# The second batch's products with w1 and w2 as seven block products per pair instead of eight

## The chip, the cores and the metric

The kernel runs on one core of one Trainium2 chip. The metric is the device time of one execution in microseconds; lower is better. Engines are named as in the profile: PE is TensorE (PEld its weight loads), DVE is VectorE, ACT is ScalarE, POOL is GpSimd, SP is SyncE, whose one queue issues every DMA.

## The reference

Attention with 16 clusters over 2 batches of 768 tokens and 8 heads, then two feed-forward layers without a softmax between them. What the change touches is the product of the attention's output x with w1 and w2 (512 by 1024 each), and what follows it:

```python
a = x @ w1                      # x is 1536 x 512: 768 rows per batch
b = x @ w2
h = a * b @ w3
x2 = h @ w_out
h2 = x2 @ w_in
g = h2 * np.clip(h2 + 3.0, 0.0, 6.0) / 6.0
return g @ w_out2
```

The kernel gets the weights as float64 and computes to float32 accuracy.

## The kernel before

Weights arrive as pairs of 32-bit words. A "conversion" (`conv_ops`, lines 691 to 727) makes float32 of 128 x 512 of them: a load of 512 KB into one of two `raw` buffers, a scaling on ScalarE (`c0`), a clamp on VectorE or GpSimd (`c1`), and three steps on VectorE (`c3`, `c4`, `c5`, lines 715, 719 and 723) into one of two `cvs` buffers.

A float32 product on PE is made of three matmuls in a rounded format: each operand is split into a rounded high part (a copy on ScalarE) and a low part (a subtraction on VectorE or GpSimd), and high·high, high·low and low·high are added in PSUM. So "a matmul of 128x384" below always comes in threes.

The program works in stages, in this order on PE. (1) Attention of both batches; into it are woven w3 times w_out (so that only one product `x2 = (a*b) @ (w3 w_out)` is left) and the first batch's products with w1 and w2 (`ab_mm`, line 838). (2) The first batch's x2 (`x2_mm`, line 955): 192 matmuls. (3) The second batch's products with w1 and w2 (`ab1_mm`, line 1006): for each of 8 column blocks `j` of 128, for two halves `hf` of the 768 tokens, for the two weights `w`, four blocks `kk` of the inner dimension, three matmuls each: 8 x 2 x 2 x 4 x 3 = 384 matmuls. ScalarE copies the product with w1 out of PSUM (`ab1_a`), VectorE multiplies the product with w2 by it (`ab1_g`, line 1017), ScalarE rounds the result and GpSimd or VectorE makes its low part (`ab1_h`, `ab1_l`). The split weights of six `j` were stored in DRAM during stage 1 (`abp`, 1 MB each) and are loaded again here; those of the last two stay in SBUF. (4) The second batch's x2, 192 matmuls. (5) The last layer in 16 panels, 8 per batch; each panel takes two column blocks of w_in as a 2 x 2 block matrix and does its product with x2 with seven block products of 6 matmuls each (`h_mm`, line 1281, Strassen's scheme in `PRO`), then 36 matmuls of 128x512 with w_out2 (`o_mm`, line 1325).

Strassen's scheme in stage 5 keeps running sums in one PSUM bank: product 0 is copied out by ScalarE (`snap`), and only then product 2 may add to that bank; after product 2 another copy, then product 4, copy, product 6; a second bank holds product 3 (copy) and product 5. So PE waits at each of these places for a copy, unless something lies between.

The order on every engine is decided at build time by a planner (`Plan.order`): each operation has durations, needs, rings of buffers it takes and drops, and a due time; the planner picks the earliest that can start, among equals the earliest due. At run time each engine works strictly through its list. `RUN_ON` says which engines an operation may use. `CV0, CVR` set the due times of the last stage's 32 conversions (16 of w_in, 16 of w_out2), whose results are stored to DRAM (`set_dram`) and fetched again by the panels.

Of the kernel before, what the change touches and what calls it, by code (L numbers as in the profile page):

```python
# [135 lines left out]
def cluster_attention_moe_kernel(  # L136
# [872 lines left out]
    def ab1_a(j, hf):  # L1009
        asb1[j, hf] = base.tile([128, HF], F32, tag="asb", name="asb", bufs=2)  # L1010
        copy_act(asb1[j, hf], W_.pop(("ab1", j, hf, 0))[:, 0:HF])

    def ab1_g(j, hf, first):
        ps, a = W_.pop(("ab1", j, hf, 1))[:, 0:HF], asb1[j, hf]
        if hf and first:
# [62 lines left out]
    CV0, CVR = 20.0, 3.4  # L1080
# [352 lines left out]
```

## Time and profile before

| | |
|---|---|
| median of 3 runs | 796.08 us (794.38 to 796.79) |
| profiled execution, its own time | 792.08 us |
| its span | 790.3 us |
| PE busy | 770.0 us (97%) |
| VectorE busy | 620.4 us (79%) |
| ScalarE busy | 510.8 us (65%) |
| GpSimd busy | 247.4 us (31%) |
| matmuls | 4519 |
| granted PE clock | full in every slice of the span |

The profiled execution took 4.0 us less than the median of the timed runs and 1.8 us more than its own span. A busy PE counts overlapping matmuls, so the rows of durations overlap; the spacing of starts is what a matmul costs in a stream.

### The profile page before, as it was taken

The numbers are of one execution on the slowest core, as the hardware profiler recorded it, in microseconds if no ns is written. First come the engines' busy times: TensorE is split into PE (matmuls) and PEld (weight loads), VectorE is DVE, ScalarE is ACT, GpSimd is POOL, SyncE is SP. The second block draws the span as 40 slices with busy tenths as digits, with TensorE's granted clock in tenths as the row PEclk, the third lists the DMA queues.
The fourth block names the chain that finished last, engine by engine and source line by source line (L and its number), as shares of the span: only waits on it lengthen the run. The fifth ranks groups of instructions, "written<-read, shape, count | busy, mean of one in ns | idle before, by whom it ended". The sixth has DMA issues, their size and how long they took to land.

```text
span 790.3 us, 12744 instructions
## 1 busy us (share of the span) xinstructions
PE 770.0 (97%) x4519; PEld 705.6 (89%) x4519; DVE 620.4 (79%) x1098; ACT 510.8 (65%) x1017; POOL 247.4 (31%) x286
## 2 busy tenths in 40 slices
PE   7799999999999999999999999999999999999998
PEld 5588887788899999999889999998889998889886
DVE  7998898999999898788985934678788676766742
ACT  5679997778877787767744522437675657555644
POOL 5733757343555454323222422211100110200100
PEclk9999999999999999999999999999999999999999
DMA  7443343333364542423346578573122213212102
GB/s 242 131 147 110 88 135 104 111 109 107 94 194 159 165 138 95 148 67 110 111 123 207 180 258 274 181 247 125 54 68 63 85 66 135 94 54 67 41 14 80
DMA packets 53135, 98.41 MB, mean 125 GB/s; under 512 B 4849, under 2 KB 31569, under 8 KB 51537
## 3 DMA queue, kind: packets, MB, share of 16 engines
q1 hardware_dynamic: 53072, 97.62, 38.8%
q8 instruction: 35, 0.57, 0.3%
q14 instruction: 28, 0.22, 0.1%
HBM read 73.43 MB, written 17.87 MB: 116 GB/s over the span
## 4 chain that ended last, share of the span: by engine, by line
PE 82%; DVE 8%; ACT 4%; issue 2%; DMA 2%; POOL 0%; SPq 0%; DVEq 0%; ACTq 0%; POOLq 0%
PE po L1325 17%; PE psh L1281 14%; PE psab L1006 8%; PE psab L838 8%; PE pst L494 7%; PE av L539 7%; PE ptr L519 7%; PE psw L769 5%; PE psx L955 4%; PE pa L388 2%; DVE cvs L719 1%; DVE den L503 1%; ACT p L511 1%; DVE pl L183 1%; PE ptkB L362 1%
## 5 line engine op out<-in xcount | busy, mean ns | idle before, releaser
L186 ACT ACTIVATE ph<-ptr 128x384 fp32r<-128x384 f32 x192 | 91.2, 487 | 44.4 <-PE ptr L519 43.3
L183 DVE TENSOR_TENSOR pl<-ptr,ph 128x384 fp32r<-128x384 f32 x192 | 103.0, 550 | 15.2 <-ACT ph L186 13.0
L503 DVE TENSOR_REDUCE den<-pst 128x1 f32<-128x768 f32 x96 | 91.2, 950 | 9.2 <-PE pst L494 7.6
L710 POOL TENSOR_SCALAR cvt<-cvt 128x512 f32<-128x512 f32 x72 | 53.9, 749 | 133.3 <-ACT cvt L186 123.8
L511 ACT ACTIVATE p<-pst,den 128x768 f32<-128x768 f32 x96 | 86.3, 898 | 9.5 <-DVE den L503 8.5
L519 PE MATMUL ptr<-id_f,p 128*128 128x128 f32 x576 | 88.9, 274 | 2.0 <-DVE pl L183 1.4
L838 PE MATMUL psab<-xT,abhl 128*128 128x384 f32 x384 | 85.7, 348 | 0.6 <-ACT asb L186 0.6
L519 PEld LDWEIGHTS ptr<-id_f,p 128*128 128x128 f32 x576 | 68.7, 140 | 12.1 <-DVE pl L183 2.3
L494 PE MATMUL pst<-kB,qB 128*128 128x512 f32 x192 | 70.3, 369 | 4.3 <-ACT p L511 4.0
L186 ACT ACTIVATE cvt<-raw 128x512 f32<-128x512 f32 x72 | 48.1, 668 | 35.5 <-DMA raw<-in_moe_w_out_dram 15.8
L539 PE MATMUL av<-ph,vs 128*128 128x384 f32 x192 | 69.7, 363 | 0.0
L838 PEld LDWEIGHTS psab<-xT,abhl 128*128 128x128 f32 x384 | 64.6, 189 | 2.5 <-ACT asb L186 1.1
L1006 PE MATMUL psab<-xT1s,abhl 128*128 128x384 f32 x384 | 66.7, 334 | 0.0
L1006 PEld LDWEIGHTS psab<-xT1s,abhl 128*128 128x128 f32 x384 | 66.6, 188 | 0.0
L494 PE MATMUL pst<-kA,qA 128*128 128x512 f32 x192 | 64.0, 338 | 0.8 <-issue 0.8
L539 PE MATMUL av<-pl,vs 128*128 128x384 f32 x192 | 64.7, 337 | 0.0
L715 DVE TENSOR_SCALAR cvs<-cvt 128x512 int32<-128x512 int32 x72 | 35.3, 492 | 27.6 <-DMA set<-cvs 21.4
L1303 ACT ACTIVATE tt<-m_sn,three 128x384 f32<-128x384 f32 x48 | 29.5, 617 | 42.2 <-DVE m_sn L1291 32.6
L186 ACT ACTIVATE m_sn<-psh 128x384 f32<-128x384 f32 x64 | 31.1, 485 | 35.8 <-PE psh L1281 35.7
L723 DVE SCALAR_TENSOR_TENSOR cvs<-cvt,cvs 128x512 int32<-128x512 int32 x72 | 53.6, 744 | 0.8
L769 PE MATMUL psw<-woh,wT 128*128 128x512 f32 x128 | 52.8, 419 | 0.0
L719 DVE SCALAR_TENSOR_TENSOR cvs<-raw,cvs 128x512 int32<-128x512 int32 x72 | 51.8, 722 | 0.9
(186 smaller groups left out, 1833.1 us busy)
## 6 DMA issues: line engine op xcount, KB each, us to landing
raw<-in_moe_w_dram SPq DMA_DIRECT2D x32, 512.0 KB, 3.8
m_gb<-set SPq DMA_DIRECT2D x64, 256.0 KB, 3.4
raw<-in_moe_w_out_dram SPq DMA_DIRECT2D x24, 512.0 KB, 3.8
raw<-in_moe_w_in_dram SPq DMA_DIRECT2D x16, 512.0 KB, 4.0
set<-cvs SPq DMA_DIRECT2D x32, 256.0 KB, 2.8
abp<-abhl SPq DMA_DIRECT2D x6, 1024.0 KB, 3.9
abhl<-abp SPq DMA_DIRECT2D x6, 1024.0 KB, 6.2
qn<-in_q_dram SPq DMA_DIRECT2D x16, 192.0 KB
```

The costliest lines, as they stand in the source:

```text
L183: nc.vector.tensor_tensor(out=out, in0=a, in1=b, op=ALU.subtract)
L186: nc.scalar.activation(out=out, in_=in_, func=AF.Copy, **kw)
L494: x = mm(out=psr[:, t, ks_], lhsT=TT["q" + nm, h][:, i, cs_], rhs=flat(TT["k" + nm, h])[:, ks_], start=st, stop=sp)
L503: done["mx", n] = [other_banks(nc.vector.tensor_reduce(out=dens[h][:, 0, c:c + 1], in_=psS[h, c], axis=AX.X, op=ALU.max, negate=True), ("S ...
L511: done["ex", n] = [other_banks(nc.scalar.activation(out=flat(p), in_=psS.pop((h, c)), func=AF.Exp, bias=d[:, 0, c:c + 1], accum_out=d[:, 1 ...
L519: nc.tensor.transpose(pt[:, blk(c)], pps[h, 3 * hf + c][:, blk(2 * s + i)], id_f)
L539: mm(out=t[:, 0:HF], lhsT=vs_t[h][:, 2 * s + i, :], rhs=x_[:, i, :], start=(s == 0 and i == 0 and n == 0), stop=(s == 2 and i == 1 and n = ...
L769: mm(out=ps, lhsT=wT[m, hf][:, a, blk(kk)], rhs=w_[hf][:, kk, :], start=(kk == 0 and n == 0), stop=(kk == 3 and n == 2))
L838: mm(out=ps[:, 0:HF], lhsT=s[:, w, a, blk(kk)], rhs=xT0[0][:, x_, kk, hf * HF:hf * HF + HF], start=(kk == 0 and n == 0), stop=(kk == KD - ...
L1006: mm(out=ps[:, 0:HF], lhsT=s[:, w, a, blk(kk)], rhs=x[:, x_, kk, hf * HF:hf * HF + HF], start=(kk == 0 and n == 0), stop=(kk == KD - 1 and ...
L1281: mm(out=ps[:, 0:HF], lhsT=left(p, l, a, kk), rhs=x[:, x_, kk, :], start=(st and kk == 0 and m == 0), stop=(kk == 1 and m == 2), skip_grou ...
L1325: mm(out=outs[b, c], lhsT=g[:, a, blk(c % 3)], rhs=w[:, w_, :], start=(first and a == 0 and w_ == 0), stop=(last and a == 1))
```

## The change

In stage 3 the two weights' column block `j` (a block of w1 and a block of w2, each cut into two halves of the inner dimension) and the second batch's x (cut into two halves of the inner dimension and two halves of the tokens) are treated as 2 x 2 block matrices and multiplied with the same seven products as in stage 5: 8 x 7 x 2 x 3 = 336 matmuls in place of 384. A "pair" below is one `j`, 42 matmuls.

For that, seven sums and differences of x's blocks are formed and split once, during stage 2 (`bx_sum`, `bx_hi`, `bx_lo`). Of the weights, float32 values are stored in stage 1 for all eight `j` (16 stores of 256 KB, straight from `cvs`) in place of six stores of split weights of 1 MB; they are fetched per pair (2 x 256 KB), four sums are formed on VectorE (`b_sum`), and seven operands are split in three pieces (`bl_hi` on ScalarE, `bl_lo` on VectorE). Out of PSUM, a pair now has four copies on ScalarE (`b_snap`), three additions on VectorE (`b_add` twice, `b_22`), and the two multiplications a*b on VectorE (`b_g0`, `b_g1`). The low part of the result is VectorE's alone (`"bl": "d"` in `RUN_ON`). The due times of the last stage's conversions move from 20 + 3.4 n to 110 + 3.9 n, behind these products; the preparation of the first batch's x2 for stage 5 moves behind them too, into stage 4. (No operation after stage 4 is itself changed.)

```diff
+    "bfs": "d", "b22": "d", "bg0": "d", "bl": "d", "bLl": "d",
...
-    ab_dram = [tc.dram_tile([128, 2048], F32, name=f"abp{j}") for j in range(J1 - 2)]
+    ab_dram = [tc.dram_tile([128, 2, 512], F32, name=f"abp{j}") for j in range(J1)]
...
+            lat=4.0 if key[0] == "set" else 2.0,
...
+    def ab_store(j, w):
+        nc.sync.dma_start(out=ab_dram[j][:, w], in_=cvo["ab", j, w])
...
+            op(("abp", j, w), "dma", 1.0, lambda j=j, w=w: ab_store(j, w), (("c5", "ab", j, w),), due=d - 0.3, lat=2.2)
             fop("abl", ("abl", j, w), {"p": 1.225, "d": 0.6}, lambda e, j=j, w=w: ab_lo(e, j, w), (("abh", j, w),),
-                due=d - 0.2, drop=("cvs",))
-        if j < J1 - 2:
-            op(("abp", j), "dma", 4.2, lambda j=j: nc.sync.dma_start(out=ab_dram[j], in_=flat2(abs_[j])),
-               (("abl", j, 0), ("abl", j, 1)), due=d + 1)
...
-                if (j, hf) in ((J1 - 2, 1), (J1 - 1, 0)):
-                    u += 0.5 if hf else -0.5
...
-    def xs_hi(kk):
-        if kk == 0:
-            xs1[0] = pool["t"].tile([128, 2, KD, S], F32R, tag="gA", name="xT1s")
-        copy_act(xs1[0][:, 0, kk, :], xT1[0][:, kk, :])
-
-    def xs_lo(e, kk):
-        sub_on(e, xs1[0][:, 1, kk, :], xT1[0][:, kk, :], xs1[0][:, 0, kk, :])
...
-    def ab1_mm(j, hf, w, kk):
-        if kk == 0:
-            bank(("ab1", j, hf, w), "psab")
-        ps, s, x = W_["ab1", j, hf, w], abs_[j], xs1[0]
-        for n, (a, x_) in enumerate(((0, 0), (0, 1), (1, 0))):
-            mm(out=ps[:, 0:HF], lhsT=s[:, w, a, blk(kk)], rhs=x[:, x_, kk, hf * HF:hf * HF + HF],
-               start=(kk == 0 and n == 0), stop=(kk == KD - 1 and n == 2))
...
+    XO = (0, 0), (1, 0), (1, 1), (0, 0), (0, 1), (1, 1), (1, 0)
+    XS = {3: ((0, 1), (0, 0)), 4: ((1, 1), (0, 1)), 5: ((1, 1), (0, 0)), 6: ((1, 0), (1, 1))}
...
+    PRO = ((0, 0, 0, True), (1, 1, 1, True), (0, 4, 5, False), (1, 5, 4, True), (0, 3, 3, False), (1, 2, 6, False),
+           (0, 6, 2, False))
...
+    def bx_sum(e, k_):
+        sub_on(e, xB(*XO[k_]), xB(*XS[k_][0]), xB(*XS[k_][1]))
+
+    def bx_hi(k_):
+        copy_act(bx[k_][:, 0], xB(*XO[k_]))
+
+    def bx_lo(e, k_):
+        sub_on(e, bx[k_][:, 1], xB(*XO[k_]), bx[k_][:, 0])
...
+    def b_fetch(j, w):
+        nc.sync.dma_start(out=bF[j % 2][:, 0:4:3] if w else bF[j % 2][:, 1:3],
+                          in_=ab_dram[j][:, w].rearrange("p (s f) -> p s f", s=2))
+
+    def b_sum(e, j, i):
+        x, y, o, g = ((0, 3, 4, ALU.add), (4, 1, 5, ALU.subtract), (1, 0, 6, ALU.subtract), (2, 5, 7, ALU.subtract))[i]
+        (nc.gpsimd if e == "pool" else nc.vector).tensor_tensor(
+            out=bF_at(j, o), in0=bF_at(j, x), in1=bF_at(j, y), op=g
+        )
...
+    def bl_hi(j, i):
+        t, f = b_part(j, i)
+        copy_act(t[:, :, 0], f)
+
+    def bl_lo(e, j, i):
+        t, f = b_part(j, i)
+        sub_on(e, t[:, :, 1], f, t[:, :, 0])
...
+    def b_mm(j, i, kk):
+        bk, l, r, st = PRO[i]
+        bk = 2 if i == 1 else bk
+        if kk == 0 and i in (0, 1, 3):
+            bank(("b", j, bk), "psab")
+        ps, t = W_["b", j, bk], bL[j % 2, l >= 3]
+        l = l if l < 3 else l - 3
+        for m, (a, x_) in enumerate(((0, 0), (0, 1), (1, 0))):
+            mm(out=ps[:, 0:HF], lhsT=t[:, l, a, blk(kk)], rhs=bx[r][:, x_, kk, :],
+               start=(st and kk == 0 and m == 0), stop=(kk == 1 and m == 2), skip_group_check=True)
...
+    def b_snap(j, i, nm):
+        t = bC[j, nm] = bs.pop(0)
+        copy_act(t, W_["b", j, PRO[i][0]][:, 0:HF])
...
+    def b_add(j, nm, i):
+        t = bC[j, nm]
+        tt(out=t, in0=t, in1=W_["b", j, 2 if i == 1 else 1][:, 0:HF], op=ALU.add)
...
+    def b_22(e, j):
+        t = bC[j, (1, 1)]
+        (nc.gpsimd if e == "pool" else nc.vector).tensor_tensor(out=t, in0=t, in1=bC[j, "s7"], op=ALU.add)
...
+    def b_g0(e, j):
+        t = bC[j, (0, 0)]
+        (nc.gpsimd if e == "pool" else nc.vector).tensor_tensor(out=t, in0=t, in1=bC[j, (1, 0)], op=ALU.mult)
...
+        tt(out=gb1[0][:, j, :], in0=bC[j, (1, 1)], in1=W_["b", j, 0][:, 0:HF], op=ALU.mult)
...
+    def b_l(e, j):
+        sub_on(e, gh1[0][:, 1, j, :], bC[j, (0, 0)], gh1[0][:, 0, j, :])
...
+    B0, BP = 33.6, 7.35
...
+                nd = [("bxl", r)] + ([("b", j, i, 0)] if kk else [("b", j, i - 1, 1)] if i else [("b", j - 1, 6, 1)] if j else
+                                     [("open", "bs")])
+                nd.append(("bll", j, 0 if l < 3 else (l - 1) // 2))
+                if kk == 0:
+                    nd += {2: [("bs", j, 0)], 4: [("bs", j, 2)], 5: [("bs", j, 3)], 6: [("bs", j, 4)]}.get(i, [])
+                end = i == 6 and kk
...
-    CV0, CVR = 20.0, 3.4
+    CV0, CVR = 110.0, 3.9
...
-        t0 = (22.0, D0 + 30.0)[b]
+        t0 = (X1 + 2.0, D0 + 30.0)[b]
```

What the change does to the lists of the engines, at three places.

VectorE in stage 3 (names: `asb`, `g1B` products of a and b, `cvs` conversions). Before, from one pair's last multiplication (`g1B`) past the next pair's two:

```order
L1017 TENSOR_TENSOR g1B<-asb,psab 128x384
L715 TENSOR_SCALAR cvs<-cvt 128x512
L719 SCALAR_TENSOR_TENSOR cvs<-raw,cvs 128x512
L723 SCALAR_TENSOR_TENSOR cvs<-cvt,cvs 128x512
L1017 TENSOR_TENSOR asb<-asb,psab 128x384
L715 TENSOR_SCALAR cvs<-cvt 128x512
L1017 TENSOR_TENSOR g1B<-asb,psab 128x384
L719 SCALAR_TENSOR_TENSOR cvs<-raw,cvs 128x512
L723 SCALAR_TENSOR_TENSOR cvs<-cvt,cvs 128x512
L715 TENSOR_SCALAR cvs<-cvt 128x512
L719 SCALAR_TENSOR_TENSOR cvs<-raw,cvs 128x512
L723 SCALAR_TENSOR_TENSOR cvs<-cvt,cvs 128x512
```

With the change, the second part of the instructions of one pair, up to the multiplication that closes it (`b_L`, `b_gv` operands from the weights, `b_sn` the copies out of PSUM, `gh1A` the low part of a*b):

```order
L184 TENSOR_TENSOR gh1A<-b_sn,gh1A 128x384
L184 TENSOR_TENSOR b_L<-b_gv,b_L 128x2x256
L1102 TENSOR_TENSOR b_sn<-b_sn,psab 128x384
L1067 TENSOR_TENSOR b_gv<-b_gv 128x256
L716 TENSOR_SCALAR cvs<-cvt 128x512
L1067 TENSOR_TENSOR b_gv<-b_gv 128x256
L720 SCALAR_TENSOR_TENSOR cvs<-raw,cvs 128x512
L1067 TENSOR_TENSOR b_gv<-b_gv 128x256
L1106 TENSOR_TENSOR b_sn<-b_sn 128x384
L1067 TENSOR_TENSOR b_gv<-b_gv 128x256
L1102 TENSOR_TENSOR b_sn<-b_sn,psab 128x384
L1119 TENSOR_TENSOR g1B<-b_sn,psab 128x384
```

A pair had 2 multiplications of its own and the rest were conversions; now it has 13 instructions of its own (four sums `b_gv`, three low parts of operands, three additions, two multiplications, one low part of the result) and about one conversion's three between them.

ScalarE in stage 3. Before (`asb` copies out of PSUM, `gh1A` the high part of the result, `cvt` a conversion's scaling):

```order
L186 ACTIVATE asb<-psab 128x384 x2
L186 ACTIVATE cvt<-raw 128x512
L186 ACTIVATE gh1A<-asb 128x384
L186 ACTIVATE asb<-psab 128x384
L186 ACTIVATE cvt<-raw 128x512
L186 ACTIVATE asb<-psab 128x384
L186 ACTIVATE gh1A<-asb 128x384
L186 ACTIVATE asb<-psab 128x384
L186 ACTIVATE cvt<-raw 128x512
L186 ACTIVATE asb<-psab 128x384
L186 ACTIVATE gh1A<-asb 128x384
```

With the change, from a pair's second and third copy on (`b_sn` copies out of PSUM, `b_w`, `b_L` high parts of the operands of the pair after the next):

```order
L187 ACTIVATE gh1A<-b_sn 128x384
L187 ACTIVATE b_sn<-psab 128x384 x2
L187 ACTIVATE cvt<-raw 128x512
L187 ACTIVATE b_sn<-psab 128x384
L187 ACTIVATE b_w_5321<-b_gv 128x3x256
L187 ACTIVATE b_L<-b_gv 128x2x256
L187 ACTIVATE b_sn<-psab 128x384
L187 ACTIVATE b_L<-b_gv 128x2x256
L187 ACTIVATE gh1A<-b_sn 128x384
L187 ACTIVATE b_sn<-psab 128x384 x3
L187 ACTIVATE cvt<-raw 128x512
```

The high part of the result `gh1A`, which waits for VectorE, now stands in the same list ahead of the copies on which PE's next products wait; before, no copy held up PE's running sum.

VectorE in stage 5, in the fourth panel. Before (`m_sn` copies out of PSUM, `tt` activations, `m_gv`, `m_whl`, `m_hl`, `m_gB` low parts, `m_gb` sums of fetched weights):

```order
L1291 TENSOR_TENSOR m_sn<-m_sn,psh 128x384
L1307 SCALAR_TENSOR_TENSOR tt<-tt,m_sn 128x384
L183 TENSOR_TENSOR m_gv<-tt,m_gv 128x384
L1182 TENSOR_TENSOR m_gb<-m_gb 128x256 x4
L1295 TENSOR_TENSOR m_sn<-m_sn 128x384
L1307 SCALAR_TENSOR_TENSOR tt<-tt,m_sn 128x384
L183 TENSOR_TENSOR m_w_5334<-m_gb,m_w_5334 128x512
L1291 TENSOR_TENSOR m_sn<-m_sn,psh 128x384
L183 TENSOR_TENSOR m_gv<-tt,m_gv 128x384
L1307 SCALAR_TENSOR_TENSOR tt<-tt,m_sn 128x384
L183 TENSOR_TENSOR x2f<-x2f 128x2x384
```

With the change, in the same panel:

```order
L1413 TENSOR_TENSOR m_sn<-m_sn,psh 128x384
L724 SCALAR_TENSOR_TENSOR cvs<-cvt,cvs 128x512
L1429 SCALAR_TENSOR_TENSOR tt<-tt,m_sn 128x384
L716 TENSOR_SCALAR cvs<-cvt 128x512
L720 SCALAR_TENSOR_TENSOR cvs<-raw,cvs 128x512
L184 TENSOR_TENSOR m_gv<-tt,m_gv 128x384
L724 SCALAR_TENSOR_TENSOR cvs<-cvt,cvs 128x512
L1311 TENSOR_TENSOR m_gb<-m_gb 128x256 x2
L1417 TENSOR_TENSOR m_sn<-m_sn 128x384
L1311 TENSOR_TENSOR m_gb<-m_gb 128x256
L716 TENSOR_SCALAR cvs<-cvt 128x512
L1429 SCALAR_TENSOR_TENSOR tt<-tt,m_sn 128x384
```

Each of the first panels now carries two conversions (`cvs`, `cvt`), where there were none. Of the 32 conversions of the last layer's weights, 5 stand before stage 2 in either list; with the change 3 stand in stage 2, 7 in stage 3, 5 in stage 4 and 12 in the first six panels of stage 5, where before none was left for stage 5.

## Rows read from the trace of the kernel before

**Rows 1.** The page, parts 1 and 4: busy time; the chain by engine.
```profile
PE 770.0 (97%) x4519; PEld 705.6 (89%) x4519; DVE 620.4 (79%) x1098; ACT 510.8 (65%) x1017; POOL 247.4 (31%) x286
...
PE 82%; DVE 8%; ACT 4%; issue 2%; DMA 2%; POOL 0%; SPq 0%; DVEq 0%; ACTq 0%; POOLq 0%
```

**Rows 2.** The chain in order of time: start us, length us, what.
```profile
434.87 66.57 PE psab L1006 x384
```

**Rows 3.** Busy us of each engine in stretches of the span.
```profile
core 0: us, PE busy (x) PEld busy (x) DVE busy (x) ACT busy (x) POOL busy (x), PEclk, DMA share, GB/s
400.50:434.80 34.30, 34.02 (x194) 33.23 (x193) 23.33 (x35) 14.74 (x24) 6.50 (x8) 1.00 0.53 162
434.80:501.30 66.50, 66.50 (x386) 66.50 (x385) 39.39 (x61) 24.22 (x43) 19.94 (x20) 1.00 0.70 229
501.30:534.50 33.20, 33.20 (x193) 33.20 (x192) 24.88 (x41) 14.88 (x23) 6.77 (x8) 1.00 0.70 229
...
550.20:644.50 94.30, 94.30 (x471) 84.93 (x470) 71.63 (x120) 59.52 (x106) 10.15 (x7) 1.00 0.22 72
```

**Rows 4.** Groups by form, 434.8 to 501.3: busy us, mean ns; idle.
```profile
L1006 PE MATMUL psab<-xT1s,abhl 128*128 128x384 f32 x384 | 66.7, 334 | 0.0
...
L180 POOL TENSOR_TENSOR gh1A<-asb,gh1A 128x384 fp32r<-128x384 f32 x8 | 11.8, 1469 | 18.4 <-ACT gh1A L186 18.4
```

**Rows 5.** Timeline of PE from 534: start, length, row, idle before.
```profile
534.55 2.24 PE L1281 MATMUL psh<-m_x,m_gB 128*128 128x384 f32 x12
...
540.51 1.32 PE L1281 MATMUL psh<-m_w,m_gB 128*128 128x384 f32 x6 [0.17 <-ACT m_sn L186]
...
542.72 2.24 PE L1325 MATMUL po<-m_w,m_whl 128*128 128x512 f32 x9
```

**Rows 6.** VectorE groups by form, 400 to 790 us.
```profile
L1182 DVE TENSOR_TENSOR m_gb<-m_gb 128x256 f32<-128x256 f32 x64 | 25.1, 420 | 0.7 <-DMA m_gb<-set 0.3
...
L723 DVE SCALAR_TENSOR_TENSOR cvs<-cvt,cvs 128x512 int32<-128x512 int32 x27 | 20.0, 741 | 0.6
L719 DVE SCALAR_TENSOR_TENSOR cvs<-raw,cvs 128x512 int32<-128x512 int32 x27 | 19.7, 732 | 0.6
L1291 DVE TENSOR_TENSOR m_sn<-m_sn,psh 128x384 f32<-128x384 f32 x32 | 17.5, 547 | 2.6 <-PE psh L1281 1.7
...
L715 DVE TENSOR_SCALAR cvs<-cvt 128x512 int32<-128x512 int32 x26 | 11.4, 439 | 26.2 <-DMA set<-cvs 21.4 <-POOL cvt L710 4.8
...
L183 DVE TENSOR_TENSOR m_hl<-m_gb,m_hl 128x512 fp32r<-128x512 f32 x7 | 4.8, 689 | 0.1
```

**Rows 7.** Timeline of VectorE from 619.6 us.
```profile
619.65 0.55 DVE L1307 SCALAR_TENSOR_TENSOR tt<-tt,m_sn 128x384 f32<-128x384 f32 x1
620.12 0.94 DVE L183 TENSOR_TENSOR x2f<-x2f 128x768 f32<-128x768 f32 x1
...
621.93 0.41 DVE L1182 TENSOR_TENSOR m_gb<-m_gb 128x256 f32<-128x256 f32 x1
622.26 0.95 DVE L183 TENSOR_TENSOR m_whl<-x2f,m_whl 128x768 fp32r<-128x768 f32 x1
623.13 0.55 DVE L183 TENSOR_TENSOR m_gv<-tt,m_gv 128x384 fp32r<-128x384 f32 x1
```

**Rows 8.** ScalarE groups by form, 434.8 to 790 us.
```profile
L186 ACT ACTIVATE m_sn<-psh 128x384 f32<-128x384 f32 x64 | 31.1, 485 | 35.8 <-PE psh L1281 35.7
...
L186 ACT ACTIVATE cvt<-raw 128x512 f32<-128x512 f32 x18 | 12.0, 669 | 22.9 <-DMA raw<-in_moe_w_out_dram 10.6 <-DMA raw<-in_moe_w_in_dram 8.3 <-DVE g1B L1017 3.6
...
L186 ACT ACTIVATE m_hl<-m_gb 128x512 fp32r<-128x512 f32 x13 | 8.1, 621 | 2.0 <-DMA m_gb<-set 1.7 <-PE po L1325 0.2
...
L186 ACT ACTIVATE m_gA<-x2f 128x768 fp32r<-128x768 f32 x4 | 3.2, 831 | 0.0
```

**Rows 9.** VectorE busy us (times) on line 723 in stretches.
```profile
0.00:400.50 400.50, 33.58 (x45) 1.00 0.42 129
...
534.50:790.00 255.50, 0.00 (x0) 1.00 0.21 72
```

More of the change, by code (lines that the diff above doesn't have):

```diff
@@ L876, in cluster_attention_moe_kernel @@
                        due=d + AR * kk / 16, take=("m",) if kk == 0 else (),
-                       drop=("hl",) if hf and w and kk == KD - 1 and j < J1 - 2 else ())
+                       drop=("hl",) if hf and w and kk == KD - 1 else ())
                 if w == 0:
@@ L888, in cluster_attention_moe_kernel @@
     op("xdone", "pe", 0.0, lambda: None,
-       [("ab", j, hf, 1, KD - 1) for j in (J1 - 2, J1 - 1) for hf in range(2)], due=105, drop=("x",))
+       [("ab", J1 - 1, hf, 1, KD - 1) for hf in range(2)], due=105, drop=("x",))
     pool, Whl = {}, []
@@ L1009, in ab1_a @@
[L1009 to L1015, printed above, removed]
+    BLK = {(i, j): (slice(2 * i, 2 * i + 2), slice(j * HF, j * HF + HF)) for i in range(2) for j in range(2)}
+    XO = (0, 0), (1, 0), (1, 1), (0, 0), (0, 1), (1, 1), (1, 0)
+    XS = {3: ((0, 1), (0, 0)), 4: ((1, 1), (0, 1)), 5: ((1, 1), (0, 0)), 6: ((1, 0), (1, 1))}
@@ new lines, in b_open_w16, with b_open_gv, b_open_hl @@
+    def b_open_w16():
+        t = base.tile([128, 4096], F32R, tag="w16", name="b_w16")
+        for i in range(2):
+            bL[i, 0] = t[:, 1536 * i:1536 * i + 1536].rearrange("p (o a f) -> p o a f", o=3, a=2)
+    def b_open_gv():
+        for _ in range(2):
+            t = pool["t"].tile([128, 1536], F32, tag="gv", name="b_gv", bufs=2)
+            bF.append(t.rearrange("p (s f) -> p s f", s=6))
+    def b_open_hl():
+        for i in range(2):
+            t = base.tile([128, 2048], F32R, tag="hl", name="b_L", bufs=2)
+            bL[i, 1] = t.rearrange("p (o a f) -> p o a f", o=4, a=2)
@@ new lines, in b_open_sn @@
+    def b_open_sn():
+        t = base.tile([128, 8, HF], F32, tag="x1b", name="b_sn")
+        for i in range(8):
+            bs.append(t[:, i])
+    allab = [("ab", J1 - 1, hf, 1, KD - 1) for hf in range(2)]
+    for nm, fn, take, need in (
+        ("bx", b_open_x, ("x",), ["xdone"]), ("bw", b_open_w16, ("w16",), [("Wl", KH - 1)]),
+        ("bg", b_open_gA, ("gA",), [("x2", 0, 0, KD - 1, J1 - 1)]), ("bh", b_open_hl, ("hl", "hl"), allab),
+        ("bv", b_open_gv, ("gv", "gv"), ["top"]), ("bs", b_open_sn, ("x1b",), [("bxl", k_) for k_ in range(7)]),
+    ):
+        op(("open", nm), "pe", 0.0, fn, need, due=-100, take=take)
@@ new lines, in xB @@
+    def xB(i, j):
+        r, c = BLK[i, j]
+        return xT1[0][:, r, c]
+    def bx_sum(e, k_):
[4 more added lines that the diff above has]
+        sub_on(e, bx[k_][:, 1], xB(*XO[k_]), bx[k_][:, 0])
+    for k_ in range(7):
+        d = T(6 + 3.5 * k_)
+        nd = [("pm", KD + i) for i in range(KD)]
+        if k_ >= 3:
+            need = {3: [("bxl", 0)], 4: [("bxs", 3)], 5: [("bxl", 2), ("bxs", 4)], 6: [("bxl", 1), ("bxs", 5)]}[k_]
+            fop("xsum", ("bxs", k_), {"d": 0.87, "p": 1.8}, lambda e, k_=k_: bx_sum(e, k_), nd + need, due=d)
+            nd = [("bxs", k_)]
+        op(("bxh", k_), "act", 0.75, lambda k_=k_: bx_hi(k_), nd + [("open", "bx" if k_ < 3 else "bg")], due=d + 0.1)
+        fop("xwl", ("bxl", k_), {"d": 0.87, "p": 1.8}, lambda e, k_=k_: bx_lo(e, k_), (("bxh", k_),), due=d + 0.2,
+            drop=("x1b",) if k_ == 6 else ())
@@ L1016, in ab1_g, with b_g1, b_h @@
+    gb1 = [None]
+    def b_g1(j):
+        if j == 0:
             gb1[0] = base.tile([128, J1, HF], F32, tag="gb", name="g1B")
-        tt(out=gb1[0][:, j, :] if hf else a, in0=a, in1=ps, op=ALU.mult)
-    def ab1_h(j, first):
-        if first:
+        tt(out=gb1[0][:, j, :], in0=bC[j, (1, 1)], in1=W_["b", j, 0][:, 0:HF], op=ALU.mult)
+        bs.append(bC.pop((j, (1, 1))))
+    def b_h(j):
+        if j == 0:
             gh1[0] = pool["t"].tile([128, 2, J1, HF], F32R, tag="gB", name="gh1A")
-        copy_act(gh1[0][:, 0, j, :], asb1[j, 0])
@@ L1057, in g1_hi @@
+    op("bend", "pe", 0.0, lambda: None, [("bl", j) for j in range(J1)] + [("bg1", j) for j in range(J1)], due=T(B0),
+       drop=("x1b",))
     def g1_hi(jp):
```

140 lines of the change are left out of this document (81 added, 59 removed).

## The prediction

> **What bounds the kernel now.** The page first: PE is busy 97% of the span and holds 82% of the chain that ended last [rows 1]. A busy share alone proves nothing, so next the chain in order of time. Through stage 3 it is one unbroken piece of PE, 384 matmuls in 66.57 us [rows 2]; that is 173.4 ns each, though one lasts 334 ns [rows 4], since they overlap. The stretches say the same: PE busy 66.50 of 66.50 us in stage 3, 33.20 of 33.20 in stage 4, 94.30 of 94.30 in six panels of stage 5; only at stage 2's start is a little idle (34.02 of 34.30) [rows 3]. So stages 2 to 5 are PE's, and a matmul less there is worth its 173.4 ns for as long as nothing else becomes late. Third, the engines beside it: in stage 3 VectorE is busy 39.39 and ScalarE 24.22 of 66.50 us; in stage 5 VectorE already 71.63 of 94.30 us [rows 3]. VectorE is the one to watch.
>
> **What is removed.** 48 of 384 matmuls: 48 x 173.4 ns = **8.3 us**; what is left takes 336 x 173.4 = 58.3 us, 7.28 us per pair.
>
> **The copies inside a pair.** Now PE may start product 2 only when product 0 has been copied, and so at four places in 42 matmuls. A product is 6 x 0.1734 = 1.04 us; a copy takes 0.485 us on ScalarE [rows 8]. Between a product's end and the one that waits lies one other product, 1.04 us of cover, so the copy may begin up to about half a microsecond late. ScalarE's pair is four copies (1.94), high parts of operands (0.83 for 768 columns, 2 x 0.62), one of the result (as a copy, 0.49) and about one conversion's scaling (0.67) [rows 8], together 5.2 of 7.28 us: enough time, but a copy can stand behind a 0.83 us operation. The nearest row is the first panel of stage 5, the only place where the seven products run today with nothing between them: from 534.55 to 542.72 us [rows 5], 8.17 us for 42 matmuls that cost 7.28, so 0.89 us lost, with a wait for ScalarE's copy shown at 540.51. There ScalarE had activations and x2's last copy as well, and VectorE stands in the way twice, since product 3 takes the bank that product 1's addition must have left; the new pair gives product 1 a bank of its own. Bounds for eight pairs: nothing (all copies under the other product) and 8 x 0.89 = 7.1 us. I take 0.3 us per pair, a third of the row because two of its causes are gone: **+2.4 us**.
>
> **VectorE in stage 3.** By the list, a middle pair has 13 instructions of its own: four sums of 256 columns (0.42 each), six of 384 columns (0.55), a low part of 768 columns (0.95) and two of 512 (0.69) [rows 6, 7], together 7.3 us, and with one conversion (0.44 + 0.73 + 0.74 = 1.91) 9.2 us. That is more than PE's 7.28. But durations are not what they cost in a row: on VectorE 384 columns of 0.55 us started 0.47 after one another, 256 columns of 0.41 gave way after 0.33, 768 columns of 0.95 after 0.87 [rows 7]; each next one starts 0.08 us before the last has ended. Sixteen of them then take 9.2 - 1.3 = 7.9 us, thirteen without a conversion 6.3. The stage's list, between the first and the last product, has 110 instructions with seven conversions: 64 us by durations, 55.5 by the spacing, against PE's 58.3. So VectorE is full but not over, because the operands of the first two pairs are made in stage 2 and those of a ninth do not exist. The worst pairs fall 0.6 us behind. That matters for one instruction: ScalarE's `gh1A`, which waits for VectorE's product, stands ahead of the copy of product 2. That copy is needed 3.1 us into the next pair, so VectorE may lag some 1.5 us before PE feels it. I take **0**; the upper bound is the sum by durations, 64 us plus the 0.7 that the first pair's multiplication comes after its last matmul, about 65 us, that is +6.7 and then instead of the copies' term.
>
> Here a rule of the Trainium skill speaks against the change. The page "VectorE: DVE Perf Modes", section "The DRAIN you can't avoid", says that the next operation does not start until the pipeline of the one before has emptied. By it VectorE's durations add up in full, and the stage would be the rival B below; the spacing in [rows 7] disagrees for operations of just this kind.
>
> GpSimd is no help and no harm there: of the low parts that it made before (1.47 us each [rows 4]) none is left to it, only the conversions' clamps.
>
> **Stages 1, 2 and 4.** Stage 1 has 16 stores of 256 KB in place of six of 1 MB, and about as many conversions in the new list as the 45 on VectorE before 400.5 us [rows 9]; the stores leave earlier in a conversion than before, so nothing queues on SP for longer. I take 0, within 1 us either way. In stage 2 VectorE gets 30 us by the spacing against 33.3 of PE, in order of need; the stage's first matmuls wait for VectorE as now. In stage 4 its list has 44 instructions, 32.4 us by durations and 28.9 by the spacing, in 33.2 us: again **0**, at most 1 us at the hand-over to stage 5, whose first panel waits for an addition that stands behind this list.
>
> **Stage 5.** Before, all conversions were done by 534.5 us [rows 9]; now 12 of 32 lie in its first six panels, two in each. VectorE was busy 71.63 / 6 = 11.9 of a panel's 15.7 us, idle 3.8 [rows 3]; two conversions less their overlaps add 2 x (1.91 - 0.24) = 3.3, so 15.3 of 15.7. If the idle time is all usable, it costs nothing. If the waits that made up those 3.8 us (for ScalarE, mostly) stay as they are, each of six panels is 3.3 us longer, 20 us. An engine that has more to do comes later to its waits and finds them over, so I am near the lower end, but the additions that free PE's bank now stand behind steps of 0.73 us: 0.3 us for each of six panels, about **+1.9 us**. The conversions are in time: 20 are done when the stage begins, enough for five panels, and two panels' worth of work brings the next panel's four, while the sixth panel's four are needed only after five panels.
>
> **The sum.** -8.3 + 2.4 + 0 + 0 + 1.9 = -4.0 us. On the profiled execution's own 792.08 us (span 790.3 and 1.8 around it) that is 788.1; that execution lies 4.0 us below the median of the runs shown, 796.08, and against this median the same difference gives **792.1 us**.
>
> **Rivals.**
> A, the forecast: the saving is kept but for a few small waits, 789 to 795 us. For it speaks that VectorE and ScalarE stay under PE by the spacing everywhere. 0.53.
> B, VectorE sets the pace in stage 3: it costs its durations there, the stage takes 65 us, and -8.3 + 6.7 + 1.9 = +0.3: 796.4 us, no change. For it: 9.2 against 7.28 us by durations, and a conversion's steps are longer still than a subtraction of as many columns (0.73 and 0.74 against 0.69 [rows 6]). Against it: rows 7's spacing. 0.20.
> C, slower: in stage 5 the waits of VectorE do not shrink. The place is the first six panels; the price, if half of the 3.8 us stays, is 15.3 + 1.9 - 15.7 = 1.5 us a panel, 8.9 us for six; -8.3 + 2.4 + 8.9 = +3.0: 799.1 us. It decides from the point where VectorE's work and remaining waits pass 15.7 us, that is from 0.4 us of waits; PE breaks even with the saving at about 1.0 us a panel. For it: VectorE's 76% without any conversion. Against it: PE waited for nothing in those panels, so there was slack in the waits. 0.14.
> D, everything is hidden: -8.3, 787.8 us. 0.13.
>
> **How the numbers follow.** About 0.3% (2.4 us) is what a measurement of this kernel can tell from no change. Faster than 793.7: four fifths of A (0.42) and D, 0.55. Within: the rest of A, most of B, a little of C, 0.30. Slower than 798.5: most of C, a little of B, 0.15. The predicted time is A's, 792.1. A's own range is 789 to 795; to leave out no more than 2 in 10 it is widened to D's 787.5 and past C's centre to 799.5.
>
> **What the profile after would show.** Stage 3 as 336 matmuls in 59 to 62 us, with short waits of PE for ScalarE's copies and none for VectorE; VectorE above 85% busy there. If B, PE's waits are in the products after `gh1A`, or for operands' low parts, and VectorE has no idle time. Stage 4 unbroken at 33.2 us. Panels of 15.7 to 16.2 us in the first six, 15.7 after. If C, the first six are 17 us and more, with PE waiting for VectorE's additions or for sets that land late. The prediction is wrong above all if ScalarE's list, where the copies stand behind operations that wait for VectorE or for a load, stops PE for longer than 0.3 us a pair.

## The result and the profile after

The change is faster: median 786.97 us (785.95 to 788.87), ratio to the kernel before 0.9901, interval 0.9877 to 0.9926. Two repeats on other occasions gave 0.9917 and 0.9913. The ratio times the 796.08 us that the prediction used is 788.2; the median itself lies 0.5 us under the stated range's lower end of 787.5.

First the page of the changed kernel, parts 1 and 4, to be read against [rows 1]:

```profile
PE 762.6 (97%) x4471; PEld 698.3 (89%) x4471; DVE 659.7 (84%) x1193; ACT 534.7 (68%) x1061; POOL 258.2 (33%) x277
...
PE 83%; DVE 9%; ACT 4%; issue 3%; DMA 1%; ACTq 0%; POOL 0%; DVEq 0%; SPq 0%; POOLq 0%
```

PE is as full as before and holds as much of the chain; VectorE went from 79% to 84%. The shares say that the character of the kernel is unchanged, not where time was won. That is in the stretches, cut at the first matmul of each stage (stages 2, 3, 4, the first panel of stage 5, the next six panels), against [rows 3]:

```profile
core 0: us, PE busy (x) PEld busy (x) DVE busy (x) ACT busy (x) POOL busy (x), PEclk, DMA share, GB/s
400.04:433.31 33.27, 33.27 (x193) 33.27 (x193) 29.49 (x46) 16.58 (x27) 8.77 (x3) 1.00 0.34 108
433.31:491.69 58.38, 58.38 (x337) 58.22 (x337) 52.52 (x106) 34.95 (x66) 11.12 (x8) 1.00 0.46 145
491.69:524.98 33.29, 33.29 (x194) 33.29 (x194) 27.41 (x44) 19.25 (x29) 14.03 (x4) 1.00 0.44 144
524.98:536.74 11.76, 9.41 (x43) 8.77 (x43) 10.49 (x19) 6.86 (x15) 1.52 (x2) 0.85 0.90 286
536.74:631.20 94.46, 94.46 (x471) 84.92 (x471) 89.85 (x152) 64.64 (x116) 19.96 (x17) 1.00 0.45 144
```

Stage 3 is 58.38 us, all of it PE's. The panels after the first take 94.46 us for six, as before, though VectorE is busy 89.85 us there, where the same six panels of before had 73.34:

```profile
542.72:637.18 94.46, 94.46 (x471) 85.05 (x471) 73.34 (x126) 60.08 (x108) 10.20 (x7) 1.00 0.21 68
```

One row of the change is new: the first panel, 11.76 us with PE busy 9.41 and a granted clock of 0.85. The next view is PE's waits from stage 3 to the end (us in total, times, longest); there are two, and both lie in that panel:

```profile
PE psh L1403 <- DVE m_sn L1413: 2.1, 1, 2.1
PE psh L1403 <- ACT m_sn L187: 0.3, 1, 0.3
```

PE's timeline there shows the wait in brackets, and behind it two rows of six matmuls that take 1.9 us from start to start in place of 1.04:

```profile
524.98 2.24 PE L1403 MATMUL psh<-m_x,m_gB 128*128 128x384 f32 x12
527.48 1.31 PE L1403 MATMUL psh<-m_x1b,m_gB 128*128 128x384 f32 x6 [0.26 <-ACT m_sn L187]
530.89 2.09 PE L1403 MATMUL psh<-m_x1b,m_gB 128*128 128x384 f32 x6 [2.10 <-DVE m_sn L1413]
532.77 2.03 PE L1403 MATMUL psh<-m_x,m_gB 128*128 128x384 f32 x6
534.64 1.22 PE L1403 MATMUL psh<-m_w,m_gB 128*128 128x384 f32 x6
535.70 1.20 PE L1403 MATMUL psh<-m_x,m_gB 128*128 128x384 f32 x6
```

Stretches of one microsecond say why (the granted clock is the third column from the end): it stays full during the wait and falls to half behind it, that is 1.2 in place of 2.4 GHz.

```profile
529.00:530.00 1.00, 0.00 (x0) 0.00 (x0) 1.00 (x2) 0.00 (x0) 0.23 (x1) 1.00 1.02 375
531.00:532.00 1.00, 1.00 (x4) 1.00 (x5) 0.66 (x3) 1.00 (x3) 0.00 (x0) 0.57 0.98 340
532.00:533.00 1.00, 1.00 (x5) 1.00 (x4) 0.68 (x2) 0.84 (x2) 0.49 (x1) 0.50 1.06 380
```

The addition that PE waited for is late because VectorE stood still for 5.37 us, 8 us earlier, at a conversion's first step that wants a result buffer whose store has not landed. VectorE's timeline:

```profile
512.74 1.28 DVE L724 SCALAR_TENSOR_TENSOR cvs<-cvt,cvs 128x512 int32<-128x512 int32 x2
513.94 1.48 DVE L184 TENSOR_TENSOR m_gB<-m_gb,m_gB 128x1280 fp32r<-128x1280 f32 x1
515.34 0.68 DVE L184 TENSOR_TENSOR m_hl<-m_gb,m_hl 128x512 fp32r<-128x512 f32 x1
515.94 0.68 DVE L184 TENSOR_TENSOR m_gB<-m_gb,m_gB 128x512 fp32r<-128x512 f32 x1
521.99 0.43 DVE L716 TENSOR_SCALAR cvs<-cvt 128x512 int32<-128x512 int32 x1 [5.37 <-DMA set<-cvs]
...
530.29 0.54 DVE L1413 TENSOR_TENSOR m_sn<-m_sn,psh 128x384 f32<-128x384 f32 x1
```

Both buffers had been finished by 514.02 us, together, and SP's queue issues their stores (L1289) only at 516.86, behind fetches (L1306, L1323) whose buffers VectorE's low parts at 513.94 and 515.34 had to free first:

```profile
515.44 0.89 SPq L1306 DMA_DIRECT2D m_gb<-set  x2
516.42 0.38 SPq L1323 DMA_DIRECT2D m_gb<-set  x1
516.86 0.90 SPq L1289 DMA_DIRECT2D set<-cvs  x2
```

So VectorE waits for a store that waits, in SP's order, for VectorE.

### The profile page after: what moved, and what is told of

It is laid out like the page before. It is cut to its first block, busy times and chain, and to the rows that moved or that the text cites. A ratio compares the mean times of both kernels' runs of the same rounds, so it can differ in the third digit from the quotient of the medians.

```text
span 785.5 us, 12835 instructions
## 1 busy us (share of the span) xinstructions
PE 762.6 (97%) x4471; PEld 698.3 (89%) x4471; DVE 659.7 (84%) x1193; ACT 534.7 (68%) x1061; POOL 258.2 (33%) x277
## 4 chain that ended last, share of the span: by engine, by line
PE 83%; DVE 9%; ACT 4%; issue 3%; DMA 1%; ACTq 0%; POOL 0%; DVEq 0%; SPq 0%; POOLq 0%
PE po L1447 17%; PE psh L1403 15%; PE psab L843 8%; PE pst L495 7%; PE av L540 7%; PE psab L1093 7%; PE ptr L520 7%; PE psw L771 5%; PE psx L956 4%; PE pa L389 3%; DVE den L504 1%; DVE pl L184 1%; DVE cvs L720 1%; ACT p L512 1%; PE ptkB L363 1%
## 5 line engine op out<-in xcount | busy, mean ns | idle before, releaser
L711 POOL TENSOR_SCALAR cvt<-cvt 128x512 f32<-128x512 f32 x72 | 75.8, 1056 | 192.6 <-ACT cvt L187 181.2
L720 DVE SCALAR_TENSOR_TENSOR cvs<-raw,cvs 128x512 int32<-128x512 int32 x72 | 49.6, 694 | 0.4
L495 PEld LDWEIGHTS pst<-kB,qB 128*128 128x128 f32 x192 | 36.1, 188 | 10.1 <-ACT p L512 7.7
L716 DVE TENSOR_SCALAR cvs<-cvt 128x512 int32<-128x512 int32 x72 | 33.5, 470 | 12.2 <-POOL cvt L711 6.7
L1447 PE MATMUL po<-m_hl,m_gv 128*128 128x512 f32 x162 | 43.7, 393 | 0.0
```

The lines of the kernel that those rows point to most:

```text
L495: x = mm(out=psr[:, t, ks_], lhsT=TT["q" + nm, h][:, i, cs_], rhs=flat(TT["k" + nm, h])[:, ks_], start=st, stop=sp)
L711: (nc.gpsimd.tensor_scalar if e == "pool" else ts)(out=tf, in0=tf, scalar1=H_MAX, scalar2=-H_MAX, op0=ALU.min, op1=ALU.max)
L1447: mm(out=outs[b, c], lhsT=g[:, a, blk(c % 3)], rhs=w[:, w_, :], start=(first and a == 0 and w_ == 0), stop=(last and a == 1))
```

## The experiments

The table has one row per profile, in us, from the starts of PE's first matmul of each stage; "rest" runs from the end of the first panel's 42 matmuls to the last matmul. Each ratio is against executions of the kernel before that were measured beside the run.

| run | median, ratio (interval) | start of stage 2 | stage 2 | stage 3 | first panel | rest | behind it |
|---|---|---|---|---|---|---|---|
| before | 796.08 | 400.42 | 34.29 | 66.56 | 8.17 | 243.89 | 3.69 |
| before_again | 793.79, 1.0001 (0.9986-1.0017) | 400.18 | 34.33 | 66.56 | 7.33 | 243.89 | 3.73 |
| before_cvs3 | 792.48, 0.9982 (0.9969-0.9995) | 400.71 | 34.32 | 66.60 | 7.35 | 243.89 | 3.65 |
| the change | 786.97, 0.9901 (0.9877-0.9926) | 400.04 | 33.27 | 58.38 | 11.76 | 243.84 | 4.92 |
| after_again | 786.21, 0.9917 (0.9899-0.9935) | 400.58 | 33.28 | 58.28 | 9.52 | 244.67 | 5.00 |
| after_third | 786.94, 0.9913 (0.9896-0.9930) | 400.95 | 33.29 | 58.38 | 10.03 | 244.55 | 4.83 |
| cvs3 | 784.80, 0.9893 (0.9873-0.9912) | 401.95 | 33.28 | 58.38 | 7.63 | 244.23 | 4.65 |
| cvs3_again | 784.86, 0.9885 (0.9865-0.9906) | 402.58 | 33.28 | 58.27 | 7.64 | 244.19 | 4.66 |
| cvs3plan | 787.28, 0.9922 (0.9901-0.9944) | 400.52 | 34.01 | 58.39 | 7.63 | 245.73 | 4.74 |
| twice | 795.03, 1.0023 (1.0001-1.0045) | 400.82 | 33.28 | 66.56 | 10.45 | 244.16 | 4.95 |
| early | 790.99, 0.9966 (0.9950-0.9983) | 400.50 | 33.28 | 58.47 | 10.49 | 246.23 | 4.62 |
| clampd | 794.06, 1.0007 (0.9992-1.0022) | 400.23 | 34.04 | 58.59 | 13.40 | 246.59 | 4.27 |
| lo3 | 804.63, 1.0131 (1.0104-1.0158) | 400.36 | 33.28 | 76.00 | 9.61 | 245.33 | 4.64 |
| lo3bh | 801.97, 1.0103 (1.0081-1.0125) | 401.97 | 33.28 | 71.37 | 12.66 | 243.78 | 4.56 |

Stage 4 takes 33.27 to 33.29 us in every row but early's (35.41).

**Both kernels again, unchanged.**

> The kernel before once more, unchanged, to see what its executions at 794 to 797 us have that the profiled one at 792.08 lacked. Theory: the 4 us are lost in one place, a late start or a stretch at a lower granted clock, so a run at 796 shows a mean clock under 1.000 or a profile with a stall that the first profile does not have; stage 3 still takes 66.4 us and the first panel of the last layer about 8.2. Rival: they are spread over stage 1 (attention), with a clock of 1.000. In either case the ratio to the kernel before is 1.000 within 0.003.

> The changed kernel once more, unchanged. If the stall at the hand-over to the last layer belongs to the change, its profile shows again VectorE waiting about 5 us for a store of a converted set near 517 us, PE waiting about 2 us for VectorE's addition in the first panel, and a stretch of some 3.5 us at the half clock behind it; first panel 11 to 12 us, stage 3 at 58.2 us without a wait. If it was one execution's bad luck, the first panel takes 8 to 9 us. Ratio 0.990 within 0.003 either way.

The stall belongs to the change: in after_again VectorE waited 4.38 us for the store and PE 1.44 us for the addition, in after_third 4.9 and 1.98 us. The half clock comes in some executions only: after_again and after_third kept the full clock in that panel, and so did *twice* with 2.10 us of wait. Of before the profile fell on a short execution (791.04 us) and shows nothing to explain the long ones; the 23 executions of before measured beside it lie between 791.5 and 797.0. before_cvs3 below bears on that.

**Product 0 twice** (each pair's product 0 is done once and once again into the same bank):

```diff
-        for m, (a, x_) in enumerate(((0, 0), (0, 1), (1, 0))):
+        for k2 in (0, 1, 0, 1) if i == 0 and kk else () if i == 0 else (kk,):
+            for m, (a, x_) in enumerate(((0, 0), (0, 1), (1, 0))):
```

> Each pair does its product 0 twice (the second overwrites the first), 48 matmuls more in stage 3 and the same list on every other engine; result unchanged. Theory (stage 3 is PE's alone): stage 3 takes 58.2 + 48 x 0.1734 = 66.5 us, and as VectorE gets 8.3 us more for the same list, the stall at the hand-over (some 4 us with the slow clock behind it) goes away: 4 to 8.3 us slower than the change, 791 to 795 us. Rival (VectorE paces stage 3 with the change): stage 3 stays under 62 us and the time within 4 us of the change's.

Stage 3 is 66.56 us, to the hundredth what 384 matmuls took before: PE alone sets that stage. But the second half of the theory fell. VectorE had 8.3 us more for the same list, and the stall at the hand-over stayed:

```profile
530.90 0.43 DVE L716 TENSOR_SCALAR cvs<-cvt 128x512 int32<-128x512 int32 x1 [5.31 <-DMA set<-cvs]
```

So it is not work left over from stage 3 that makes the addition late; the wait between two of VectorE's instructions in stage 4 is there all the same.

**A third result buffer, lists unchanged.**

```diff
-            s = cvo[key] = base.tile([128, 512], I32, tag="cvs", name="cvs", bufs=2)
+            s = cvo[key] = base.tile([128, 512], I32, tag="cvs", name="cvs", bufs=3)
```

> A third buffer for the conversions' results, every engine's list unchanged. Theory (VectorE's 5.4 us wait for a store of a set makes the first panel's addition late): the wait shrinks to about 1.5 us (then it is the clamp of the next conversion that ends it), PE waits under 0.5 us in the first panel and keeps its full clock, the panel takes 7.5 to 8.3 us in place of 11.8; 3.5 to 4 us faster than the change, about 783 us, ratio 0.984 to 0.986. Rival (VectorE has too much work in stage 4, or GpSimd's slow clamps make it late whatever the buffers): VectorE's wait moves elsewhere, the panel stays over 10.5 us, and the time stays within 1 us of the change's.

> The third buffer again, lists unchanged, to say whether it beats the change. Theory: first panel 7.4 to 8.3 us, 2 to 4 us less than in the change; stage 1 gives back nothing (the 1 to 2 us that its first profile had more there were that execution's), so 783 to 785 us, 2 to 3 us under the change in the same call. Rival: the buffer moves what lies in memory and stage 1 is 1 to 2 us longer each time: 785 us, within 1.5 us of the change.

The wait shrank to 1.40 us, and what ends it is GpSimd's clamp, as expected. PE's panel has no wait left:

```profile
519.94 0.43 DVE L716 TENSOR_SCALAR cvs<-cvt 128x512 int32<-128x512 int32 x1 [1.40 <-POOL cvt L711]
```

```profile
526.89 2.25 PE L1403 MATMUL psh<-m_x,m_gB 128*128 128x384 f32 x12
529.05 2.35 PE L1403 MATMUL psh<-m_x1b,m_gB 128*128 128x384 f32 x12
531.25 1.21 PE L1403 MATMUL psh<-m_x,m_gB 128*128 128x384 f32 x6
532.33 1.31 PE L1403 MATMUL psh<-m_w,m_gB 128*128 128x384 f32 x6
533.48 1.20 PE L1403 MATMUL psh<-m_x,m_gB 128*128 128x384 f32 x6
```

The panel falls from 9.5 to 11.8 us to 7.63, and the store is shown to be the cause. The median gains 1.4 us the first time and 2.1 the second, less than the 3.5 to 4 expected: stage 1 is 1.0 to 2.5 us longer in both profiles, as the rival of the second run had it. In both, the stretch 20 to 60 us has a granted clock of 0.96, in after_third 1.00, with the same waits of PE ahead of it. Whether the buffer has a part in that is open; before_cvs3 and cvs3plan, with three buffers too, have 1.00 there. Of the twelve executions of cvs3 and cvs3_again, the six with a mean clock of 0.999 or 1.000 took 783.1 to 784.4 us, the other six, both profiled ones among them, 785.2 to 786.0. By its median this is the fastest version, though the interval of its ratio still overlaps with the change's.

**The third buffer in the kernel before** (the same edit).

> The kernel before with a third buffer for the conversions' results, every engine's list unchanged. In before VectorE waits 21 to 23 us for stores of sets, eight times, up to 5.7 us each, and PE in the profiles for next to nothing of it. Theory (half of before's executions, at 794 to 797 us, lose their 2 to 4 us where one of those waits becomes a stall of PE in the first panel): with the third buffer the slower executions go, median 791.5 to 792.5 and clock 1.000 in nearly all, ratio 0.997 to 0.998. Rival (the spread comes from elsewhere, or such a wait costs PE nothing): median and spread as before, ratio 1.000 within 0.0015, slower executions still there.

The long executions went: 12 lie between 791.0 and 793.6 us, the 23 of before beside them between 792.0 and 796.3. The clock of 1.000 in nearly all did not come: five of the 12 have 0.997 or 0.998, but the longest took 793.6 us. VectorE has more waits for stores in before than in the change, where there is one (us in total, times, longest); most cost PE nothing. First before_again, then before_cvs3:

```profile
DVE cvs L715 <- DMA set<-cvs: 22.6, 8, 5.7
```

```profile
DVE cvs L715 <- POOL cvt L710: 18.3, 12, 4.2
...
DVE cvs L715 <- DMA set<-cvs: 3.1, 1, 3.1
```

The waits for stores shrink to 3.1 us, while those for the clamps grow from 4.4 to 18.3. So what before loses in its long executions goes with the number of buffers; that it goes through a store's wait that becomes a stall of PE is argued, since no profile caught a long execution.

**More work for VectorE in stage 3** (the subtraction of 768 columns three times), and **the same with ScalarE's order changed** (high part of a result behind the next pair's copy of product 2):

```diff
-        sub_on(e, t[:, :, 1], f, t[:, :, 0])
+        for _ in range(1 if i else 3):
+            sub_on(e, t[:, :, 1], f, t[:, :, 0])
...
+                   after=[("bs", j + 1, 2)] * (j < J1 - 1),
```

> Each pair's subtraction of 768 columns on VectorE is done three times (same result): 16 subtractions more in all, by their spacing 16 x 0.87 = 13.9 us, 12 of them (10.4 us) within stage 3. Theory (by the spacing VectorE had 52.5 us of work in stage 3's 58.2 and holds PE up as soon as it has more): stage 3 takes 61 to 65 us, PE waits there for VectorE or for ScalarE's copies behind it, the time is 3 to 8 us above the change's. Rival (operands are made a pair or two ahead, so VectorE's lateness is taken up and PE feels nothing): stage 3 stays under 59.5 us and the time within 2 us of the change's.

> The overloaded stage 3 once more (two more subtractions of 768 columns per pair), but ScalarE's high part of a pair's result now stands behind the next pair's copy of product 2. Theory (PE's waits there came from the copies standing behind that operation, which waits for VectorE): stage 3 takes 62 to 69 us in place of 76, down to VectorE's own work of about 66, and keeps the full clock; 8 to 12 us less than without the reordering. Rival (PE waits because VectorE's additions and operands are late, whatever ScalarE's order): stage 3 still takes 73 us or more.

Stage 3 grows by 17.6 us for 10 to 14 us of work, more than the theory allowed. Waits in stage 3 of lo3, then of lo3bh:

```profile
PE psab L1094 <- ACT b_sn L187: 10.2, 8, 2.9
ACT gh1A L187 <- DVE b_sn L1112: 9.4, 7, 5.5
ACT b_L L187 <- DVE b_gv L1067: 6.9, 8, 2.0
```

```profile
ACT b_L L187 <- DVE b_gv L1067: 13.5, 10, 3.6
...
PE psab L1094 <- ACT b_sn L187: 9.6, 6, 2.3
```

PE waits 10.2 us for ScalarE's copies, which stand behind operations that wait for VectorE, among them `gh1A`, which the prediction named. Most of the other 7.4 us is clock: the stage's mean is 0.93 (third column from the end; 1.00 in the change), by an estimate from these rows 0.07 x 76.0 = 5.3 us. First lo3, then lo3bh:

```profile
433.64:509.64 76.00, 65.76 (x337) 62.59 (x337) 66.25 (x121) 35.02 (x66) 7.46 (x9) 0.93 0.38 120
```

```profile
435.25:506.62 71.37, 61.72 (x337) 59.48 (x337) 66.42 (x119) 34.96 (x66) 6.27 (x9) 0.98 0.39 122
```

With `gh1A` out of the way PE's waits hardly shrink (9.6 us), because the high parts of operands `b_L`, which had waited 6.9 us for VectorE's sums already, now wait 13.5. Neither expectation held (71.4 us lies between 69 and 73). Of the 4.6 us that the stage is shorter, waits are 0.6 and most of the rest is the higher clock, one profile each; and as the first panel is 3.1 us longer, the medians differ by only 2.7. In both variants ScalarE, which works through its list in order, passes VectorE's lateness on to PE.

**The due times of before** (`CV0, CVR = 20.0, 3.4`).

> The change with the due times of before for the last layer's conversions (20 + 3.4 n): by its list 10 conversions stand in stage 3 (7 with the change), 6 in stage 4 (5) and 8 in the first three panels (12 in seven). Theory (a store of a set that VectorE waits for in stage 4 is what costs, and PE has slack elsewhere): stage 3 at 58.2 to 59.5 us though VectorE has 5.6 us more there, the first panel late again (over 9 us), the time within 2 us of the change's. Rival (the later due times are what kept VectorE under PE): stage 3 at 61 us or more, PE waiting there, the time over 3 us above the change's.

Neither held as a whole. Stage 3 stays at 58.47 us with three conversions more by the list, so PE really had that slack, and the first panel is late again; but the run is 4 to 5 us above the change. The first panel (10.49 us) is no longer than the change's: stage 4 takes 2.1 us more and the panels behind the first 1.9. Waits of PE from 492 us on (one of the first line's two, 0.62 us, lies in a later panel):

```profile
PE psh L1403 <- ACT m_sn L187: 1.8, 2, 1.2
PE psx L956 <- DVE gh1A L184: 1.7, 1, 1.7
PE psh L1403 <- DVE m_sn L1413: 1.4, 1, 1.4
```

In stage 4, x2's matmuls wait 1.7 us for the result's last low part. It stands behind VectorE's additions and conversions, and it also took 1.77 us where the one before it, at 492.85, took 0.60, while GpSimd made a low part beside it (VectorE, then GpSimd):

```profile
496.26 1.77 DVE L184 TENSOR_TENSOR gh1A<-b_sn,gh1A 128x384 fp32r<-128x384 f32 x1
```

```profile
493.38 4.23 POOL L181 TENSOR_TENSOR m_x<-x2f,m_x 128x768 fp32r<-128x768 f32 x1 [1.26 <-ACT m_x L187]
```

So, by an estimate from these rows, some 1.2 us of that wait are the slow instruction and not the number of conversions; in the change VectorE makes `m_x`. The later due times are worth 4 to 5 us, behind the stage where I expected them.

**Two more variants around the buffer.**

> The third buffer made known to the planner too, so that lists change a little: one conversion fewer in the first panels, none in the seventh. Theory: like the third buffer alone, 783 to 786 us, first panel 7.4 to 8.3 us, stage 3 at 58.2. Rival (the planner puts a third conversion right ahead of the first panel's operands, and VectorE is late by its own work): first panel over 9 us and 786 us or more.

> The change with the clamps of the last layer's conversions on VectorE, 32 instructions of about 0.43 us more there and none of them on GpSimd, where two took 12.8 us in stage 4. Two buffers as in the change. Theory (the store of a set behind the fetches on SP's queue makes VectorE late): VectorE waits again 4 us or more for a store near the end of stage 4, first panel over 9 us; 786 to 790 us. Rival (the slow clamps bunch the conversions, and without that the stores are spread out): no wait for a store over 2 us there, first panel under 8.5 us, 783 to 785.5 us.

With the third buffer known to the planner the first panel is as short, but stage 2 and the panels lose 0.7 and 1.5 us; it is no better than the change. With the clamps on VectorE the rival fell: the wait for the store is there again, 5.08 us, and the panel is the longest of all. The time expected was missed too: 794.06 us, 7 us above the change, with 3.0 us more in the first panel, 2.2 in the others and 0.8 in stage 2. As this variant also gives VectorE 32 x 0.43 = 13.8 us more work, it shows that slow clamps are not needed for the wait, not what the panel would take without them.

```profile
524.96 0.43 DVE L716 TENSOR_SCALAR cvs<-cvt 128x512 int32<-128x512 int32 x1 [5.08 <-DMA set<-cvs]
```

## Why the prediction was right, and where it was off

The direction and the main mechanism were right. By its own terms, with means over three profiles of the change and two of before:

- **Removed matmuls, -8.3 us:** 66.56 to 58.35, -8.2. Right, and *twice* shows that the stage is PE's alone.
- **Copies inside a pair, +2.4:** measured 0; PE waits nowhere in stage 3. The step that failed is the choice of a third of the first panel's loss in [rows 5]. In before_again and before_cvs3 that panel takes 7.33 and 7.35 us with the same seven products, so even for this pattern the row overstated the cost; what made it 8.17 us in the first profile is not shown beyond the wait of 0.17 us.
- **VectorE in stage 3, +0:** right. It was busy 52.52 of 58.38 us, 90%, where the list by spacing gave 55.5. The groups of its durations there add up to 60.8 us, more than the stage is long, with 6 us of idle time besides; so rival B's price, the sum by durations, is excluded. Its mechanism showed as soon as VectorE got more work (lo3). The Trainium skill, page "VectorE: DVE Perf Modes", section "The DRAIN you can't avoid", taken as a rule for every pair of operations, disagrees with these rows; the section's first paragraph ends by pointing to another ("Two Vector instructions with no wait between them") by which an operation starts earlier where nothing holds it, and with that the trace agrees.
- **Stages 1, 2 and 4, +0 within 1 us:** stage 1 is 0.2 us longer; stage 2 is 1.0 us shorter, all at its start, where before PE's matmuls come as VectorE's low parts of `gh` are ready, 13 in 3.17 us (before_again, first two rows), and with the change 29 in 5.19 us (third row, a fence of its own).

```profile
400.18 3.01 PE L955 MATMUL psx<-gh,Whl 128*128 128x384 f32 x13
403.35 1.86 PE L955 MATMUL psx<-gh,Whl 128*128 128x384 f32 x9 [0.16 <-DVE gh L183]
```

```profile
400.04 5.19 PE L956 MATMUL psx<-gh,Whl 128*128 128x384 f32 x29
```

Stage 4 is as forecast (33.28). The hand-over "at most 1 us" is the step that failed most: the first panel takes 10.4 us in the mean, 2.7 more than before. I had counted VectorE's list (28.9 us by the spacing in 33.2) and not what its instructions wait for: a store that is issued 2.8 us after its data is ready and lands 5 us later.
- **Panels of stage 5, +1.9:** apart from the first, +0.5 for all of them. Rival C is excluded: VectorE took up 16.5 us more work in six panels, and its waits there shrank from 20.5 to 5.5 us.
- **Not foreseen:** +1.2 us behind the last matmul (0.6 to 1.2 in the variants). The final stores land later there (2.6 us in the median against 2.1 in before), and an instruction fetch of two packets stands in that stretch, which before does not have; DMA queues and issues from 775 us on:

```profile
q14 instruction: 2, 0.02, 0.7%
...
out_dram<-osb SPq DMA_DIRECT2D x6, 256.0 KB, 2.6
```

Which of the two it is was not tried.

The sum of these is -4.7 us by spans, where I forecast -4.0; so errors of 2.4, 1.4 and 1.0 us one way and 2.7 and 1.2 the other cancelled; that the sum came out so near is luck. The median lies near rival D's 787.8 us, but not by its mechanism: the first panel's stall is not hidden. Between medians the change gains 6.6 to 8.9 us. What is beyond the 4.7 us comes from the kernel before: its profiled executions, on which the sum was made, are among its shortest, and I carried the same difference over to its median. before_cvs3 shows what this hides: 0.18% (0.05 to 0.31) of before goes with its two buffers. With the third buffer on both sides the ratio is, by an estimate from separate runs, 0.9889 / 0.9982 = 0.991 (0.9889 is the mean of the two runs).

Not tried: the stores on another queue, or ahead of the fetches, so whether the late issue or the slow landing is the larger part of the 5.37 us stays open; and in before the stall itself was never caught in a profile.

## What to carry to other kernels

Here, where one engine was unbroken, removed work was worth its full price, and the losses came at the seams: look at the last instructions ahead of a new stage and at what each waits for, DMA landings and queue order included, not only at their durations. A sum of an engine's work against its room says nothing about a wait in the middle of its list; the same lists with one more buffer showed what that wait cost. Check whether the profiled execution is a typical one before a difference is carried over to the median.
